# Softmax decode attention, forward and backward, on one core: the number of parts in which V of the first two head pairs is loaded

## The chip, the core and the metric

The kernel runs on one core of a Trainium2 chip. The metric is the device time of one execution in microseconds (us). The core has a matrix engine (PE, whose weight loads are listed as PEld), a vector engine (DVE), a scalar engine (ACT), a general engine (POOL) and a sync engine (SP) that here does nothing but start transfers. Transfers between the chip's main memory (DRAM, HBM) and the on-chip buffers are carried by 16 DMA engines.

## What is computed

One query row per head attends to 8192 keys, and the gradients of that are returned as well:

```python
B, H, Sq, Skv, Dh = 1, 32, 1, 8192, 128          # all bf16

def _fwd_reference(q, k, v):
    scale = q.shape[-1] ** -0.5
    scores = jnp.einsum('bhqd,bhkd->bhqk', q, k) * scale
    attn = _softmax(scores, axis=-1)
    return jnp.einsum('bhqk,bhkd->bhqd', attn, v)

def reference(q, k, v, grad_out):
    _out, _vjp = jax.vjp(_f, q, k, v)      # _f is _fwd_reference
    return (_out, *_vjp(grad_out))         # out, dq, dk, dv
```

K and V are read (134 MB together) and dK and dV, which have the same size, are written. dK is the outer product of the gradient of the scores (a number per key) with q, dV that of the softmax weights with grad_out.

## The kernel before

The 32 heads are taken as 16 pairs. K of a pair, 4 MB, lies in one buffer `Kt` of 128 partitions by 128 slots by 128 numbers; a slot is 256 bytes, so each partition holds 32 KB. V lies in the same way in `Vt`. There are three buffers for K (`K_BUFS`) and two for V (`V_BUFS`). The results overwrite the inputs: line 290 writes dV of a pair into its V buffer and dK into its K buffer, and stores carry the buffers to DRAM. A buffer is loaded again only when its stores have landed.

For each pair j the loop from line 355 on makes the scores with K (`k_blocks`, `k_scores`), the softmax, dK of the pair before, and then in eight steps r over sixteen slots each: transposes of V (`v_transposes`, line 215), the product of the softmax weights with V (`contract`, line 265), and dV (`outer`, line 290).

Transfers by the SP engine are issued in the order of the program: an issue that has to wait holds up all behind it. The order at the start is K of pair 0 (K0) in four parts, V0 in two, K1 in one, V1 in four, K2 in two (`LOADS`, lines 25 and 98 to 102). Then come the store of the second half of dV of pair 0 (line 299), the store of dK of pair 0 (line 305), the load of V2 (line 93; it goes into the buffer of V0, so it waits for all of dV of pair 0 to be stored), the two halves of dV of pair 1, and the load of K3. From there on it is one load and one store in turn, 4 MB each.

A transfer of 128 partitions is cut into packets of one partition each: 32 KB when the pair's buffer is moved in one part, 16 KB for a half, 8 KB for a quarter. Each of the 16 DMA engines has eight partitions of it.

The first half of dV of pair 0 (the slots below `SHARED`) is not stored by SP but by POOL, through a second queue (q0 in the profile; SP's is q1). `share_out` (lines 116 to 121) starts six stores, one for each entry of `SHARES`: the first engine, the first partition and the number of partitions, every third of them, in pieces of 8 KB. Before each it starts a tiny transfer (`turned`, line 111) that moves the place at which the next store begins among the engines. The entries give the 16 engines different amounts: between none and 24 pieces of 8 KB.

```python
def share_out(dst, src):
    for engine, first, n in SHARES:
        turn_to(engine)
        last = first + 3 * n - 2
        nc.gpsimd.dma_start(dst[first:last:3], src[first:last:3], max_dma_last_dim=8192)
```

Of the kernel before, what the change touches and what calls it, by code (L numbers as in the profile page):

```python
# [21 lines left out]
K_BUFS = 3  # L22
V_BUFS = 2
QD = 32
LOADS = {("k", 0): 4, ("v", 0): 2, ("v", 1): 4, ("k", 2): 2}
SHARED = 64
SHARES = ((6, 12, 39), (5, 2, 42), (5, 1, 8), (15, 55, 25), (10, 25, 10), (7, 0, 4))
GP = 4
# [3 lines left out]
def kernel(  # L32
# [50 lines left out]
    def load_k(j):  # L83
        parts = LOADS.get(("k", j), 1)
        Kt[j] = kpool.tile([P, NT, D], BF16, tag="K", name="Kt")
        for c in range(parts):
            nc.sync.dma_start(slots(Kt[j], c, parts), rows_of(k, j, c, parts))

    def load_v(j):
        Vt[j] = vpool.tile([P, NT, D], BF16, tag="V", name="Vt")  # L90
        parts = LOADS.get(("v", j), 1)
        for c in range(parts):
# [432 lines left out]
```

## Time and profile before

| what | value |
|---|---|
| time, median of 3 runs | 632.92 us (632.18 to 633.14) |
| time of the profiled execution | 632.87 us |
| its span on the core | 631.1 us |
| PE busy | 462.9 us (73%) |
| DVE busy | 516.4 us (82%) |
| ACT busy | 205.1 us (32%) |
| DMA traffic | 268.98 MB in 12164 packets, mean 426 GB/s |
| read from and written to HBM | 134.23 MB each |

The span is the time from the first to the last event that the profiler records on the core; the time of the execution is 1.8 us longer. Lines of the profile name the engine, the line of the program (L93 is line 93), the operation, and what is written from what (`Vt<-in_v_dram` is a load of V). "SPq" and "POOLq" are the sequencers that start transfers.

### The profile page before, as it was taken

To read this page: it belongs to the slowest core of one execution; us is meant where nothing else is said; L and a number is where in the kernel's file an instruction comes from. 1 tells how busy PE (TensorE), PEld (TensorE's weight loads), DVE (VectorE), ACT (ScalarE), POOL (GpSimd) and SP (SyncE) were. 2 spreads that over 40 slices of the span, in tenths; PEclk is the share of its full clock that TensorE was granted. 3 is DMA by queue.
4 is the path that set the end of the run, shared out by engine and by line. 5 is a ranking of instruction groups with operands and counts; after the bars stand their busy time and mean duration, and the time that the engine had idled before them with its cause. 6 is when DMAs were issued, how large, how long until landed. Compare 5 with 4: busy or idle time off the path is not lost.

```text
span 631.1 us, 8018 instructions
## 1 busy us (share of the span) xinstructions
PE 462.9 (73%) x3256; PEld 245.9 (39%) x3256; DVE 516.4 (82%) x654; ACT 205.1 (32%) x460; POOL 11.3 (2%) x23
## 2 busy tenths in 40 slices
PE   4887678878787788676888757867679776697671
PEld 1443344244443425233363432624336243262441
DVE  6579997989889798796879959879697895987973
ACT  2432424043342505134052330613316142160431
POOL 2040000000000000000000000000000000000000
PEclk9789987789798977788868789777897778987785
DMA  8999999999999999999999999999999999999997
GB/s 366 433 402 436 430 428 431 429 427 440 433 427 436 436 431 433 433 432 429 429 432 429 427 433 427 433 432 418 431 430 437 436 431 425 436 427 431 428 426 336
DMA packets 12164, 268.98 MB, mean 426 GB/s; under 512 B 1856, under 2 KB 1888, under 8 KB 1888
## 3 DMA queue, kind: packets, MB, share of 16 engines
q1 hardware_dynamic: 11232, 266.34, 98.5%
q0 software_dynamic: 800, 2.12, 0.8%
q8 instruction: 25, 0.41, 0.2%
q14 instruction: 11, 0.09, 0.0%
q10 hardware_dynamic: 96, 0.02, 0.0%
HBM read 134.23 MB, written 134.23 MB: 425 GB/s over the span
## 4 chain that ended last, share of the span: by engine, by line
issue 91%; DMA 3%; PE 3%; DVE 1%; ACT 0%; POOL 0%; POOLq 0%; ACTq 0%
DMA out_dram<-Vt 2%; PE s_ps L198 1%; DMA Kt<-in_k_dram 1%; PE T_ps L215 1%; PE acc_p L265 0%; DVE XK_sb L188 0%; DVE Vt L290 0%; POOL out_dram L120 0%; DVE q_blk L174 0%; ACT p_rep L452 0%; DVE sT L205 0%; ACT win L255 0%; ACT e L440 0%; POOL turned L111 0%; POOLq L520 0%
## 5 line engine op out<-in xcount | busy, mean ns | idle before, releaser
L198 PE MATMUL s_ps<-XK_sb,q_win 128*128 128x512 bf16 x512 | 152.4, 432 | 66.6 <-DVE XK_sb L188 61.3
L290 DVE TENSOR_TENSOR Vt<-p_rep,qd 128x2048 bf16<-128x2048 bf16 x128 | 154.0, 1223 | 40.1 <-PE acc_p L265 32.2
L188 DVE STREAM_TRANSPOSE XK_sb<-Kt 128x1024 f32<-128x1024 f32 x128 | 150.2, 1218 | 37.7 <-DMA Kt<-in_k_dram 35.0
L215 PE MATMUL T_ps<-ident_f,Vt 128*128 128x128 f32 x1024 | 165.4, 314 | 6.1 <-DMA Vt<-in_v_dram 6.1
L220 ACT COPY XV_sb<-T_ps 128x512 f32<-128x512 f32 x256 | 139.6, 591 | 82.6 <-PE T_ps L215 82.4
L290 DVE TENSOR_TENSOR Kt<-ds_rep,qd 128x2048 bf16<-128x2048 bf16 x128 | 149.5, 1215 | 3.2 <-PE acc_ds L265 2.8
L215 PEld LDWEIGHTS T_ps<-ident_f,Vt 128*128 128x128 f32 x1024 | 131.2, 160 | 43.8 <-issue 18.7
L198 PEld LDWEIGHTS <-q_win 128*128 128x128 bf16 x512 | 51.6, 110 | 155.6 <-issue 123.9
L265 PE MATMUL acc_p<-Vt,win 128*32 128x512 bf16 x512 | 55.9, 439 | 2.8 <-ACT win L255 2.8
L440 ACT ACTIVATE e<-sT,nbias 128x128 f32<-128x128 f32 x16 | 8.2, 515 | 150.6 <-DVE nbias L436 150.6
L265 PEld LDWEIGHTS <-win 128*32 128x32 bf16 x1024 | 23.0, 99 | 60.6 <-issue 49.4
L265 PE MATMUL acc_ds<-Kt,win 128*32 128x512 bf16 x512 | 42.7, 429 | 4.6 <-ACT win L255 4.6
L232 PE MATMUL dp_ps<-XV_sb,do_win 128*32 128x512 bf16 x512 | 34.3, 383 | 13.5 <-ACT XV_sb L220 13.5
L255 ACT COPY win<-ds 64x128 bf16<-64x128 bf16 x32 | 9.5, 296 | 106.4 <-DVE ds L327 106.2
L232 PEld LDWEIGHTS <-do_win 128*32 128x32 bf16 x512 | 14.3, 94 | 29.2 <-issue 22.5
L441 PE MATMUL m_ps<-rs,ones_f 128*128 128x1 f32 x32 | 7.5, 305 | 24.4 <-ACT e L440 24.4
L427 PE MATMUL m_ps<-ident_f,top 128*128 128x128 f32 x16 | 4.8, 300 | 23.5 <-DVE top L425 23.5
L205 DVE STREAM_TRANSPOSE sT<-s_ps 128x512 f32<-128x512 f32 x16 | 11.5, 717 | 10.7 <-PE s_ps L198 10.7
L441 PEld LDWEIGHTS m_ps<-rs,ones_f 128*128 128x128 f32 x32 | 6.2, 242 | 27.6 <-ACT e L440 27.6
L452 ACT ACTIVATE p_rep<-e,rinv 128x512 bf16<-128x512 f32 x16 | 11.5, 722 | 13.3 <-DVE rinv L450 13.3
L427 PEld LDWEIGHTS m_ps<-ident_f,top 128*128 128x128 f32 x16 | 2.1, 133 | 31.0 <-issue 25.4
L317 PEld LDWEIGHTS m_ps<-pd,ones_f 128*128 128x128 f32 x32 | 8.2, 276 | 10.6 <-DVE prod L248 9.8
(60 smaller groups left out, 158.1 us busy)
## 6 DMA issues: line engine op xcount, KB each, us to landing
Kt<-in_k_dram SPq DMA_DIRECT2D x14, 4096.0 KB, 29.1
Vt<-in_v_dram SPq DMA_DIRECT2D x14, 4096.0 KB, 29.0
out_dram<-Kt SPq DMA_DIRECT2D x13, 4096.0 KB, 25.1
out_dram<-Vt SPq DMA_DIRECT2D x13, 4096.0 KB, 32.3
out_dram<-Vt SPq DMA_DIRECT2D x5, 2048.0 KB, 16.2
out_dram<-Kt SPq DMA_DIRECT2D x5, 2048.0 KB, 15.7
Kt<-in_k_dram SPq DMA_DIRECT2D x4, 1024.0 KB, 8.2
Vt<-in_v_dram SPq DMA_DIRECT2D x2, 2048.0 KB, 17.5
```

What stands on the lines that cost most here:

```text
L188: nc.vector.transpose(XK[j, u][:].rearrange("p g w i -> p (g w i)"), slots(Kt[j], u, NU).rearrange("p g d -> p (g d)").bitcast(F32))
L198: nc.tensor.matmul(st[j]["s"][:], lhsT=q_win[:, c, at:at + P], rhs=cols[:, c // 2, c % 2], start=(u == 0 and c == 0), stop=(u == NU - 1 an ...
L205: nc.vector.transpose(sT[:].rearrange("p g r -> p (g r)"), x["s"][:])
L215: nc.tensor.transpose(T_ps[:, i, :], words[:, m * P:(m + 1) * P], ident_f[:])
L220: nc.scalar.copy(XV[j][:, b * TB:(b + 1) * TB, :], st[j].pop(("T", c))[:])
L232: nc.tensor.matmul(out[b * QD:(b + 1) * QD, :], lhsT=do_win[:, b // 2, e2, at:at + QD], rhs=cols[:, z, e2, :, b * QD:(b + 1) * QD], start= ...
L255: nc.scalar.copy(win[t * M:(t + 1) * M, :, at:at + 4], src[t * M:(t + 1) * M])
L265: nc.tensor.matmul(acc[which][b * QD:(b + 1) * QD, :], lhsT=win[:, g, at:at + QD], rhs=X[:, 4 * g:4 * g + 4, :].rearrange("p n d -> p (n d)"),
L290: nc.vector.tensor_tensor(slots(G, r, NU).rearrange("p n (a b) -> p n a b", b=R), slots(rep, r, NU).unsqueeze(2).to_broadcast([P, CH, D // ...
L317: nc.tensor.matmul(x["m"][:, 1:3], lhsT=ones_f[:], rhs=x["pd"][:], start=True, stop=True, skip_group_check=True)
L441: nc.tensor.matmul(x["m"][:, 0:1], lhsT=ones_f[:], rhs=rs[:], start=True, stop=True, skip_group_check=True)
L452: nc.scalar.activation(x["p"][:], e[:].unsqueeze(2).to_broadcast([P, NT, R]), ACT.Copy, scale=rinv[:])
```

## The change

```diff
-LOADS = {("k", 0): 4, ("v", 0): 2, ("v", 1): 4, ("k", 2): 2}
+LOADS = {("k", 0): 4, ("v", 0): 4, ("v", 1): 2, ("k", 2): 2}
```

V0 is loaded in four quarters (512 packets of 8 KB) where it was two halves (256 of 16 KB), and V1 in two halves where it was four quarters. The number of transfers, of packets and of bytes of the two together stays what it was. The order of the instructions on PE, DVE, ACT and POOL is the same; on SP the two loads exchange their numbers of issues, so that the single issue of K1 comes two issues later.

## The prediction, made before the changed kernel had run

> **What bounds the kernel now.** I read the page first: the row of DMA and the queue table.
>
> ```profile
> DMA  8999999999999999999999999999999999999997
> GB/s 366 433 402 436 430 428 431 429 427 440 433 427 436 436 431 433 433 432 429 429 432 429 427 433 427 433 432 418 431 430 437 436 431 425 436 427 431 428 426 336
> q1 hardware_dynamic: 11232, 266.34, 98.5%
> ```
>
> The 16 DMA engines are full in all slices but the first and the last; no other engine is (DVE, the next, has 82%). I also added up the trace's packet records, which give queue, start, duration and size: after the first packets at 2.0 us no engine is idle until the first has finished everything at 626.6 us. So the time is the DMA work. Moving work between other engines costs nothing, and an idle microsecond on the DMA engine that finishes last costs one microsecond. The 16 engines end between 626.6 and 630.1 us (the completion marks of the last stores); span 631.1, time 632.87, 0.05 below the median of the runs.
>
> Second, the order of SP's issues and what they wait for, because the engines stay full only while SP issues in time:
>
> ```profile
> 38.77 0.35 SPq L299 DMA_DIRECT2D out_dram<-Vt  x1
> 52.89 0.34 SPq L305 DMA_DIRECT2D out_dram<-Kt  x1
> 65.04 0.34 SPq L93 DMA_DIRECT2D Vt<-in_v_dram  x1
> 73.17 4.87 SPq L305 DMA_DIRECT2D out_dram<-Vt  x2
> 78.14 0.67 SPq L87 DMA_DIRECT2D Kt<-in_k_dram  x1
> ```
>
> ```profile
> SPq L93 <- DMA out_dram<-Vt: 11.7, 3, 6.1
> ```
>
> These are the times of issue, and from the table of waits (50 to 80 us) the line of V loads. V2's load goes out at 65.04 after a wait for stores of dV of pair 0 (dV0). Ahead of it in the queue there is then nothing but the store of dK of pair 0 (dK0, issued at 52.89). Behind it on SP stand the two halves of dV1 and the load of K3.
>
> Third, the DMA issues up to 60 us with their time to landing:
>
> ```profile
> out_dram<-Kt SPq DMA_DIRECT2D x1, 4096.0 KB, 21.9
> out_dram<-Vt SPq DMA_DIRECT2D x1, 2048.0 KB, 26.2
> ...
> out_dram<-Vt POOLq DMA_DIRECT2D x1, 64.0 KB, 17.3
> ```
>
> SP's half of dV0 lands at 38.77 + 26.2 = 65.0: this releases V2. POOL's last share, issued at 45.80, lands at 63.1, only 1.9 us before. dK0 lands at 74.8, and it covers V2's issue. A transfer of 64 KB that takes 17 us is the line to stop at. Why so long is seen in the queue counts of two windows, 37 to 48 us and 49 to 58 us:
>
> ```profile
> q1 hardware_dynamic: 382, 3.20, 69.8%
> q0 software_dynamic: 380, 1.45, 32.3%
> ```
>
> ```profile
> q1 hardware_dynamic: 233, 3.41, 89.0%
> q0 software_dynamic: 226, 0.42, 12.0%
> ```
>
> q0 is POOL's queue, q1 SP's (packets, MB, share). Whether SP's packets are mostly 8 KB (V1, first window) or 16 KB (K2, second), there is about one packet of q0 for each of q1, while the bytes are far from equal. So the engines take the two queues in turn, packet by packet: the share-out's pace is one packet per packet of SP. Larger packets on SP slow it.
>
> **The change part by part.** *V0 in four parts.* SP's issues early on each wait for the landing of the transfer eight before (the waits of K1 on the q row, of V1's parts on the grad row and three parts of K0, of K2 on K0 and V0). With two more issues ahead, K1 would go out at about 5.8 instead of 4.24, when K0's first part has landed, V1 at 8.2 and 10.6, K2 at 13.1 and 15.5. K0 and V0 keep the queue full until 22.8, so all are in time. PE takes V0 from 20.73 on and its second half from 31.98, and shows no wait for it. Price 0; the cover is some 17 us of queued work. Packets of 8 KB take 0.309 us, of 16 KB 0.611: 256 more here and 256 fewer in V1 cancel.
>
> *V1 in two parts* has the same zero for its users: the first half is used at 46.49 and has landed by 39.7, or a bit earlier with the change. But it is what SP's queue moves when the share-out begins. Step by step, per DMA engine:
>
> Before. POOL's first packet begins at 36.2; 12.4 of V1's 32 packets have begun by then (199 over 16 engines). Left on q1 until dV0's half is done: 19.6 of V1, 16 of K2, 8 of dV0 = 43.6. POOL's queue holds 256 pieces of 8 KB and 368 of 4 bytes (marks and fillers; a record of 8 bytes goes with one of these) = 624, or 39 turns. In the records from 36.2 to 59 us there are 613 packets of q1 to 585 of these: 1.05 each, so 39 turns take 41 packets, 2.6 short of 43.6; three 16 KB packets (1.83 us) do lie between the last mark of q0 (63.01) and the last of dV0's half (64.84). The count fits.
>
> After. The same bytes of V1 have moved at 36.2, that is 6.2 of 16 packets. Left until the end of dV0's half: 9.8 + 16 + 8 = 33.8. The share-out needs 39 to 41, so 5.2 to 7.2 turns are left, and what is next on q1 is dK0 with 32 KB packets of 1.213 us. I take 5.7, nearer the lower end, since some of the 5% are moments in which q0 was not ready for 0.3 us, which a packet of 0.6 us hides. POOL's two last shares wait for the first two to land (41.53 and 45.80 now) and go out about 2 and 5 us later, while some 15 turns still stand in the queue; no price.
>
> So on the engines with most of the share-out, whose part of dV0's half ends at 64.8 in both kernels (the same work in another order), the share-out ends at 64.8 + 5.7 x 1.22 = 71.8. V2's load is issued 0.2 later, 72.0, instead of 65.04. Its first packet comes 1.4 after the issue, as for the first K load (issued 0.74, first packets 1.99 to 2.6): 73.4.
>
> The cover: dK0's sixteen completion marks lie at 67.5, 70.5, then eleven from 71.3 to 73.0 and four from 74.4 to 74.6. The first to be done is the engine with nothing of the share-out. It would stand idle from 67.5 to 73.4, 5.9 us, the next 2.9, most 0.4 to 2.1, the last four not at all. What is late next: dV1's first store (73.17) stands behind V2 and is just not held up. PE's transposes of V2 wait 0.4 us for its landing at 84.2, which the last engines set; these lose nothing.
>
> What 5.9 us on one engine cost at the end: I followed its marks from transfer to transfer. It takes 9.70 to 10 us for most 4 MB transfers where the others take 9.68, so its lead of 3 us is gone by about 345 us, and it ends at 629.1, 1.0 before the last. The sum: 5.9 - 1.0 = 4.9 us later. Against the profiled time 632.87 + 4.9 = **637.8 us**. Nothing wins it back: no DMA engine is idle later.
>
> Bounds: each turn more or less is 1.22 us. With 4 turns 635.7; with 7.2 639.6; if all eight packets of dK0 pass first, 640.6, and about a microsecond more if the first packets after the stop are as long as the first of the run (0.6 to 1.1 us for 0.31). With 2.8 turns 634.2, 0.2% above 632.87; with 1.7 nothing is left.
>
> The Trainium skill (DMA: Bandwidth & Descriptors, "Queues, rings and completion order") says that a DMA engine changes between queues after a whole packet of typically 9 to 17 descriptors. By that the 39 turns would be through in three to five changes, the size of SP's packets would not matter, and the sum would be 632.9. The two windows above, with as many packets of q0 as of q1, speak against it, unless the 1:1 is chance.
>
> **The rivals.** (a) *The share-out isn't paced by SP's packets*: its 1:1 comes from how fast POOL's pieces become ready, about one in 0.6 us per engine. Then it still ends at about 63, dV0's half releases V2 at 65, and the time is 632.9. For it: 0.62 us is the turn in both windows (0.309 + 0.309 with data, 0.611 with a mark). Against: in the second window the pieces are nearly all marks of some 9 ns, long issued, and still wait one 16 KB packet each. It decides from 2.8 turns down; this is the case on the other side, not slower.
>
> (b) *The stretch in which stores set in gets cheaper.* From 30 to 40 us the rate is 377 and 374 GB/s instead of some 430: 1.3 us lost, with V1's packets at 0.42 us on the mean from about 35 to 37 us. If that is a cost per packet, half as many save half, 0.6 us; with (a) this gives 632.3, at most 631.6. Against: the bytes in flight are the same.
>
> (c) *The share-out outlasts dK0* on some engine: V2 goes out at about 75, all engines run dry, dV1's stores and K3 come late with it, 641 us. For it: engines with 41 or more turns exist in the records (three packets left there, up to six elsewhere).
>
> That the change doesn't change the packets can be excluded: the parts are separate issues of 8192 and 4096 numbers per partition.
>
> **Chances.** Forecast 0.73, (a) 0.12, (b) 0.05, (c) 0.10. The forecast's own range is 635.7 to 639.6 (4 to 7.2 turns). For 8 in 10 I go on to 640.6 at the top (eight turns), and down to 634.2 (2.8 turns), where (a) begins. About 0.2% (1.3 us) is what a measurement of this kernel can tell from no change; (a) and most of (b) lie within. Faster 0.03, the same 0.14, slower 0.83.
>
> **What would show it.** In the profile after: V2's load (L93) issued at 70 to 74 instead of 65.04, its wait for dV0's stores longer by that, with POOL's last share landing last; q0 packets in the window 66 to 72, where there were none; POOL's shares 5 and 6 issued at about 43.5 and 51; DMA share below 0.9 somewhere in 68 to 76, and 16 completion marks at the end spread over 8 us instead of 3.5, with a lower last slice. Wrong it would be if V2's issue stays at 65, or if it moves and the end does not (then some engine's idle time was free).

## The result, and the profile after

The changed kernel takes 638.97 us (median of 6 runs, 636.35 to 639.55) where the kernel before, run beside it, takes 632.69 (6 runs, 632.18 to 633.18): ratio of the means 1.0088, 95% interval 1.0073 to 1.0102. The profiled execution took 639.43 us with a span of 637.6.

The page of the changed kernel, the same rows:

```profile
DMA  8999999999999999999999999999999999999995
GB/s 362 430 418 431 384 396 430 437 425 438 429 435 428 427 433 434 429 434 429 433 427 434 429 432 429 429 438 427 439 426 433 430 427 431 434 439 429 420 422 241
q1 hardware_dynamic: 11232, 266.34, 97.7%
```

Traffic and packets are what they were. The rate is lower in two places: the fifth and sixth slice (64 to 96 us: 384 and 396 GB/s) and the last (241 instead of 336). The row of tenths hides the first of them.

Two words for what follows. A mark is the record of 4 bytes with which a transfer ends on an engine, so each transfer has 16. Times of packet records and marks, here and in the prediction, are counted from a zero 0.24 us before that of the rows of issues; differences between records are not touched by it.

SP's issues, and the wait of V2's load:

```profile
39.03 0.35 SPq L299 DMA_DIRECT2D out_dram<-Vt  x1
53.14 0.34 SPq L305 DMA_DIRECT2D out_dram<-Kt  x1
71.22 0.34 SPq L93 DMA_DIRECT2D Vt<-in_v_dram  x1
73.63 4.87 SPq L305 DMA_DIRECT2D out_dram<-Vt  x2
78.60 0.39 SPq L87 DMA_DIRECT2D Kt<-in_k_dram  x1
```

```profile
SPq L93 <- DMA out_dram<-Vt: 17.5, 1, 17.5
```

Of these issues one has moved by more than 0.5 us: V2's, by 6.2 us. Its wait has grown from 11.7 to 17.5 us. What it waits for is seen in the transfers issued up to 60 us (size, time to landing) and in POOL's last two shares:

```profile
out_dram<-Kt SPq DMA_DIRECT2D x1, 4096.0 KB, 21.6
out_dram<-Vt SPq DMA_DIRECT2D x1, 2048.0 KB, 26.0
...
out_dram<-Vt POOLq DMA_DIRECT2D x1, 400.0 KB, 25.8
...
out_dram<-Vt POOLq DMA_DIRECT2D x1, 64.0 KB, 20.6
```

```profile
42.76 0.56 POOL L120 DMA_DIRECT2D out_dram<-Vt  x1 [5.59 <-DMA out_dram<-Vt]
...
50.46 0.59 POOL L120 DMA_DIRECT2D out_dram<-Vt  x1 [5.86 <-DMA out_dram<-Vt]
```

SP's half of dV0 lands at 39.03 + 26.0 = 65.0, as before. POOL's last share, issued at 50.46, lands at 71.1, where it was 63.1: the share-out now releases V2. dK0 lands at 53.14 + 21.6 = 74.7, as before, but V2 is no longer queued behind it in time. The queue counts from 66 to 72 us show the share-out beside dK0's 32 KB packets, and the windows after it the hole (columns: window, length, busy time and number of instructions of five engines, granted clock, DMA share, GB/s):

```profile
q1 hardware_dynamic: 71, 2.06, 79.9%
q0 software_dynamic: 38, 0.05, 2.6%
```

```profile
66.00:70.00 4.00, 2.52 (x27) 1.01 (x25) 2.85 (x5) 2.98 (x8) 0.00 (x0) 0.65 0.95 406
70.00:72.00 2.00, 2.00 (x16) 0.82 (x8) 2.00 (x3) 0.34 (x1) 0.00 (x0) 0.50 0.63 258
72.00:74.00 2.00, 2.00 (x14) 1.58 (x10) 2.00 (x3) 0.83 (x2) 0.00 (x0) 0.50 0.91 279
```

In the kernel before, q0 has no packet in this stretch and the three windows moved 426, 463 and 401 GB/s. From 72 to 74 us the engines are 91% busy and move 279 GB/s: V2's first packets are slow. In the packet records, 13 of the packets that begin from 72.4 to 74.8 take 1.7 to 2.2 us instead of 1.21.

### The profile page after: what moved, and what is told of

Same layout as the page of the kernel before. It is cut to its first block, busy times and chain, and to the rows that moved or that the text cites. A ratio compares the mean times of both kernels' runs of the same rounds, so it can differ in the third digit from the quotient of the medians.

```text
span 637.6 us, 8018 instructions
## 1 busy us (share of the span) xinstructions
PE 463.3 (73%) x3256; PEld 247.8 (39%) x3256; DVE 516.2 (81%) x654; ACT 205.1 (32%) x460; POOL 11.1 (2%) x23
## 4 chain that ended last, share of the span: by engine, by line
issue 90%; DMA 3%; PE 3%; DVE 1%; ACT 0%; POOL 0%; POOLq 0%; ACTq 0%
DMA turned<-in_k_dram 3%; PE s_ps L198 1%; DMA Kt<-in_k_dram 1%; PE T_ps L215 1%; PE acc_p L265 0%; POOL out_dram L120 0%; DVE XK_sb L188 0%; DVE Vt L290 0%; DVE q_blk L174 0%; ACT p_rep L452 0%; DVE sT L205 0%; ACT win L255 0%; ACT e L440 0%; POOL turned L111 0%; POOLq L520 0%
## 5 line engine op out<-in xcount | busy, mean ns | idle before, releaser
L198 PE MATMUL s_ps<-XK_sb,q_win 128*128 128x512 bf16 x512 | 154.1, 438 | 69.3 <-DVE XK_sb L188 64.5
L265 PE MATMUL acc_ds<-Kt,win 128*32 128x512 bf16 x512 | 41.3, 417 | 4.6 <-ACT win L255 4.6
```

The costliest lines, as they stand in the source:

```text
L198: nc.tensor.matmul(st[j]["s"][:], lhsT=q_win[:, c, at:at + P], rhs=cols[:, c // 2, c % 2], start=(u == 0 and c == 0), stop=(u == NU - 1 an ...
L265: nc.tensor.matmul(acc[which][b * QD:(b + 1) * QD, :], lhsT=win[:, g, at:at + QD], rhs=X[:, 4 * g:4 * g + 4, :].rearrange("p n d -> p (n d)"),
```

## The experiments

Each kernel was timed beside the kernel before; the ratio is to that. The issue time of V2's load comes from the one profiled execution of each kernel.

**Which part of the change.** V1 alone:

```diff
-LOADS = {("k", 0): 4, ("v", 0): 2, ("v", 1): 4, ("k", 2): 2}
+LOADS = {("k", 0): 4, ("v", 0): 2, ("v", 1): 2, ("k", 2): 2}
```

> V1 alone in two parts, V0 in two as before. Turn theory (POOL's store queue moves one packet for each packet of SP's queue, so V1's fewer packets leave about six turns to the 32 KB packets of dK0, V2's load goes out at 70 to 73 us, the engine without share-out work stands idle some 6 us): like the changed kernel, 636 to 640 us. Rival (the finer V0, which pushes K1's issue back by 2.4 us, has a part in it): V2's load is issued 1 us or more earlier than at 71.2 and the time is 634 to 636 us.

640.07 us (637.14 to 640.96), ratio 1.0108 [1.0083, 1.0133]; V2's load at 72.51. Not to be told from the changed kernel.

V0 alone:

```diff
-LOADS = {("k", 0): 4, ("v", 0): 2, ("v", 1): 4, ("k", 2): 2}
+LOADS = {("k", 0): 4, ("v", 0): 4, ("v", 1): 4, ("k", 2): 2}
```

> V0 alone in four parts, V1 in four as before. Turn theory: V2's load at 65.0 us, no engine idle, 632 to 633.5 us, no change. Rival (the finer V0 has a part in it): V2's load later than 66 us, 634 us or more.

633.24 us, ratio 1.0006 [0.9996, 1.0015]; V2's load at 65.11. The finer V0 costs nothing that can be measured; V1 alone makes the loss.

**Is it the packets that SP's queue moves beside the share-out?** The changed kernel with K2 in four parts, so that V1 keeps its large packets and K2 makes up for their number:

```diff
-LOADS = {("k", 0): 4, ("v", 0): 4, ("v", 1): 2, ("k", 2): 2}
+LOADS = {("k", 0): 4, ("v", 0): 4, ("v", 1): 2, ("k", 2): 4}
```

> The changed kernel with K2 in four parts of 8 KB packets instead of two of 16 KB. Turn theory: packets left on SP's queue when the share-out begins are 9.8 of V1, 32 of K2 and 8 of dV0's half, 49.8 and more than the 39 to 41 turns of the share-out, so it ends in good time before dV0's half; V2's load at about 65 us, 632 to 633.5 us: the loss is gone although V1 stays in two parts. Rival (something in V1's two parts themselves, their landing or the later issue of K1): V2's load stays at 70 us or later and the time at 636 to 640 us.

633.09 us, ratio 1.0008 [0.9998, 1.0017], and V2's load goes out in time:

```profile
65.48 0.34 SPq L93 DMA_DIRECT2D Vt<-in_v_dram  x1
```

The loss is gone with V1 still in two parts. The opposite, K2 in one part and V1 untouched:

```diff
-LOADS = {("k", 0): 4, ("v", 0): 2, ("v", 1): 4, ("k", 2): 2}
+LOADS = {("k", 0): 4, ("v", 0): 2, ("v", 1): 4, ("k", 2): 1}
```

> The kernel before with K2 in one part of 32 KB packets instead of two of 16 KB; V0 and V1 untouched. Turn theory: 19.6 packets of V1, 8 of K2, 8 of dV0's half are left, 35.6, so 3.4 to 5.4 turns go to dK0's packets; V2's load at 69 to 71.5 us, the first engine idle 3 to 5 us, with the slow first packets of a restart (about 1.6 us in the changed kernel) 635 to 639 us. Rival (the loss comes with V1's parts): no change, 632 to 633.5 us.

637.00 us, 635.12 to 640.88 in six runs, ratio 1.0077 [1.0046, 1.0108]. The loss comes without touching V1. The profiled execution, one of the shortest (635.28 us), has V2's load some 1.5 us earlier than expected:

```profile
67.48 0.34 SPq L93 DMA_DIRECT2D Vt<-in_v_dram  x1
```

Why this kernel varies by 5.8 us, more than any other here, was not settled: only one of its executions has a trace.

A larger dose, V1 in one part of 32 KB packets:

```diff
-LOADS = {("k", 0): 4, ("v", 0): 2, ("v", 1): 4, ("k", 2): 2}
+LOADS = {("k", 0): 4, ("v", 0): 2, ("v", 1): 1, ("k", 2): 2}
```

> The kernel before with V1 in one part of 32 KB packets. Turn theory: 4.9 packets of V1, 16 of K2 and 8 of dV0's half are left when the share-out begins, 28.9, so 10 to 12 turns would have to go beside dK0, which has only eight packets: the share-out outlasts dK0 on every engine, V2's load goes out at 74.5 to 76 us, the first engine is idle some 9 us and all others too, 640 to 644 us, more than the changed kernel. Rival (the delay comes with the change from four parts to fewer and has one size): 636 to 640 us, V2's load at 70 to 73 us.

643.84 us, ratio 1.0175 [1.0160, 1.0190]. Its issue of V2 and its windows:

```profile
75.49 0.34 SPq L93 DMA_DIRECT2D Vt<-in_v_dram  x1
```

```profile
72.00:74.00 2.00, 1.60 (x22) 0.57 (x22) 2.00 (x3) 0.85 (x3) 0.00 (x0) 1.00 0.28 98
74.00:76.00 2.00, 2.00 (x11) 0.87 (x10) 2.00 (x2) 0.34 (x2) 0.00 (x0) 1.00 0.00 0
```

Here all 16 engines stand still for two microseconds, as expected where the share-out outlasts dK0.

**Turns or bytes?** The same question from POOL's side: larger pieces in the changed kernel, smaller ones in the kernel before.

```diff
-            nc.gpsimd.dma_start(dst[first:last:3], src[first:last:3], max_dma_last_dim=8192)
+            nc.gpsimd.dma_start(dst[first:last:3], src[first:last:3], max_dma_last_dim=16384)
```

> The changed kernel with the share-out cut into pieces of up to 16 KB instead of 8 KB; the same bytes go to the same DMA engines. Turn theory: with half as many pieces the share-out needs some 25 turns per engine instead of 39, fewer than the 33.8 packets left on SP's queue, so V2's load goes out at about 65 us and the time is 632 to 634 us. Rival (the share-out is late because of its bytes, or because SP's larger packets take a larger share of the bytes): V2's load at 70 us or later, 636 to 640 us.

V2's load goes out at 64.86, in time; and the kernel takes 639.09 us, ratio 1.0102 [1.0085, 1.0118]. The step up to V2 held, the time did not. The records have 128 pieces and 48 fillers (records of 4 bytes in the place of a piece), 11 per engine where 14 were expected, so the pieces do not lie on the engines they were on. A second try changed all entries but the longest:

```diff
-            nc.gpsimd.dma_start(dst[first:last:3], src[first:last:3], max_dma_last_dim=8192)
+            nc.gpsimd.dma_start(dst[first:last:3], src[first:last:3], max_dma_last_dim=8192 if n == 25 else 16384)
```

> The changed kernel with pieces of up to 16 KB in all entries of the share-out but the one of 25 partitions, which keeps its 8 KB pieces; with 16 KB throughout that entry had come to lie on other DMA engines (11 pieces and fillers per engine where 14 were expected), so V2's load was in time (64.9 us) and one engine still ended 5 us behind. Turn theory: 30 turns per engine instead of 39, fewer than the 33.8 packets left on SP's queue, V2's load at about 65 us; and since every entry now gives the same engines the same bytes as in the kernel before, also 632 to 634.5 us. Rival (larger pieces cost the lead of that engine in some other way): V2's load at 65 us and 637 to 640 us. Rival (bytes, not turns, make the share-out late): V2's load at 68 us or later.

637.66 us, ratio 1.0081 [1.0066, 1.0096], V2's load at 65.96: the first rival. The trace does not name the engines, but one of them can be followed: its packets are regularly a little longer than the others' (below). In the kernel before it is the first of the 16 to finish the first half of dV1, with its mark at 82.2 us. With 16 KB throughout that mark lies at 88.7, and here at 87.0, or 6.5 and 4.8 us later; the two kernels take 6.3 and 4.7 us longer. It has lost its lead to the pieces, not to waiting, and in both kernels one engine ends late: in the second, the last marks are fifteen at 630.0 to 630.3 and one at 634.4. So the expectation that every entry would keep its engines most likely failed too. That is inferred: in the kernel before this engine, as far as its records can be followed, has 39 of 4 bytes in the share-out and not one piece, and 4.8 us are about eight packets of 16 KB at 0.611 us.

The clean test of turns against bytes therefore goes the other way, with pieces cut smaller in the kernel before and every piece where it was:

```diff
-            nc.gpsimd.dma_start(dst[first:last:3], src[first:last:3], max_dma_last_dim=8192)
+            nc.gpsimd.dma_start(dst[first:last:3], src[first:last:3], max_dma_last_dim=4096)
```

> The kernel before with the share-out in pieces of 4 KB instead of 8 KB; the loads are untouched, each entry keeps its partitions, its order and its DMA engines (39 x 4 x 2048 numbers where it was 39 x 2 x 4096). Turn theory: 56 turns for pieces and fillers instead of 28, and 11 others, 67 per engine, against 43.6 packets left on SP's queue up to the end of dV0's half and eight of dK0: the share-out outlasts dK0, V2's load goes out at 74 to 77 us, and the time is 639 to 645 us, as with V1 in one part. Rival (the share-out's bytes, or SP's large packets as such, set its end): V2's load at 65 to 67 us, 632 to 635 us.

643.16 us, ratio 1.0164 [1.0147, 1.0181], with the same loads and the same bytes. V2's issue, and the queues from 49 to 58 us:

```profile
75.17 0.34 SPq L93 DMA_DIRECT2D Vt<-in_v_dram  x1
```

```profile
q1 hardware_dynamic: 245, 3.52, 92.1%
q0 software_dynamic: 245, 0.28, 8.7%
```

Again about one for one (both counts take in records of 4 bytes). Bytes are ruled out: halving the pieces delays V2 as much as quartering V1's number of packets does.

**What is the lead of one engine worth?** The kernel before without the share-out, so that all engines get the same:

```diff
-SHARED = 64
+SHARED = 0
```

> The kernel before without the share-out: SP stores all of dV of pair 0 in one transfer, so POOL's queue has no store to wait for and all 16 engines get the same work. Theory of the leading engine (one DMA engine loses some 7 us on the others over the run and needs its lead of up to 5 us from the share-out): V2's load without delay by the share-out, no engine idle, and yet 636 to 638 us, with one engine ending some 5 us after most others. Rival (the lead has no worth; the changed kernel loses by the dry stretch as such, on all engines): 632 to 634 us.

636.44 us, ratio 1.0059 [1.0044, 1.0074]; V2's load at 63.95 and, by the packet records, the engines idle for 0.2 us each in all from 5 to 600 us. It loses 3.7 us nevertheless: eleven engines end at 627.7 to 629.4, three by 630.8, the last two at 632.2 and 633.1. The last windows:

```profile
625.00:630.00 5.00, 0.00 (x0) 0.00 (x0) 0.00 (x0) 0.00 (x0) 0.00 (x0) 0.50 0.69 291
630.00:635.00 5.00, 0.00 (x0) 0.00 (x0) 0.00 (x0) 0.00 (x0) 0.00 (x0) 0.50 0.05 23
```

The control, the changed kernel without the share-out:

```diff
-SHARED = 64
+SHARED = 0
```

> The changed kernel without the share-out: SP stores all of dV of pair 0. Turn theory: with nothing on POOL's queue, V1's packets hold nothing up, so it is as the kernel before without the share-out (636.4 us): 635.5 to 637.5 us, V2's load at about 64 us. Rival (V1 in two parts costs something by itself): 638 us or more.

636.52 us, ratio 1.0060 [1.0043, 1.0077], V2's load at 64.43: the same as without the share-out before. No cost of V1 in two parts is seen without POOL's queue beside it.

All of it by one count (left: packets of SP's queue per engine from the start of the share-out to the end of dV0's half, worked out as in the prediction; turns: those of the share-out; slow engine: its mark at the end of dV1's store, in the profiled execution, whose time stands behind it):

| kernel | turns | left | V2's load issued, us | slow engine, us | profiled, us | median, us |
|---|---|---|---|---|---|---|
| before | 39 | 43.6 | 65.04 | 87.3 | 632.87 | 632.69 |
| V0 in four | 39 | 43.6 | 65.11 | 87.5 | 633.18 | 633.24 |
| changed, K2 in four | 39 | 49.8 | 65.48 | 87.9 | 632.82 | 633.09 |
| changed, 16 KB pieces | 22 | 33.8 | 64.86 | 93.8 | 638.91 | 639.09 |
| changed, mixed pieces | 30 | 33.8 | 65.96 | 92.0 | 637.36 | 637.66 |
| before, K2 in one | 39 | 35.6 | 67.48 | 89.9 | 635.28 | 637.00 |
| changed | 39 | 33.8 | 71.22 | 94.0 | 639.43 | 638.97 |
| V1 in two | 39 | 33.8 | 72.51 | 95.1 | 640.96 | 640.07 |
| V1 in one | 39 | 28.9 | 75.49 | 98.2 | 643.47 | 643.84 |
| before, 4 KB pieces | 67 | 43.6 | 75.17 | 98.0 | 643.26 | 643.16 |
| before, no share-out | - | - | 63.95 | 91.3 | 635.99 | 636.44 |
| changed, no share-out | - | - | 64.43 | 91.6 | 636.44 | 636.52 |

V2 is late in just the kernels with more turns than packets left. The two with the larger pieces lose for the other reason, the place of the work among the engines. The column of the slow engine joins the two reasons. This engine is known in every trace by the load behind dV1: at least six of its eight packets of 32 KB there are longer than 1.213 us, and of any other engine at most two. In all twelve profiled executions the time is 544.7 to 545.8 us more than its mark, while the times themselves differ by up to 10.7 us. So the loss of each kernel is already there when this one engine is done with dV1. No kernel tried was faster than the one before.

## Why the prediction was right, and what it mis-sized

The forecast was 637.8 us; the median is 638.97 and the profiled execution 639.43. The mechanism is the one forecast, and the experiments above confirm its two halves separately. That the number comes so close is in part luck: V2's first packets begin at 72.4 instead of 73.4, 1.0 us too early for the sum, and this hides more than half of the 1.9 us by which slow packets were left out of it.

- *V0 in four parts, price 0*: shown by the run with V0 alone. K1's issue came at 6.66, not at about 5.8, without effect.
- *One packet for one packet*: 5.7 turns left over was a little high, though within the range given. The last mark of the share-out lies at 71.0, and (71.0 - 64.8) / 1.22 = 5.1. V2's load went out at 71.22 instead of 72.0.
- *The first engine idle for 5.9 us*: its part of dK0 ends at 66.8, and V2's first packets begin at 72.4: 5.6 us. (Of dK0's sixteen marks before, ten and not eleven lie from 71.3 to 73.0; nothing in the sum hangs on it.)
- *The restart*: this is the term that was too small. I let V2 start at full speed and put slow first packets, as about a microsecond, into the upper bound alone. V2's marks lie at 84.0 to 87.0 instead of 77.2 to 84.3. From 72.4 a 4 MB transfer at 9.70 us would end on the first engine at 82.1, so slow packets cost it 1.9 us more. From 40 to 90 us packets took 1.9 us per engine more above their usual 0.31, 0.61 and 1.21 than in the kernel before. About 0.7 of that comes with V2's first packets, 1.1 with its last ones: at 80.5 to 84.2 us, just before the engines pass to dV1's store, nine of them within 0.3 us, some thirty packets take 1.35 to 2.5 us. Both groups are in all four kernels in which most engines ran dry (changed, V1 in two, V1 in one, 4 KB pieces), 0.6 to 0.7 and 1.1 to 1.2 us per engine. With K2 in one part, where one engine alone stood idle, some 1.5 us, the last group is 0.3; in the other kernels no 4 us from 60 to 100 us have more than 0.12. So the slow last packets go with the dry stretch as well; why packets become slow in either place, no run shows.
- *The last four engines lose nothing*: wrong for the same reason; their marks of V2 come 2.0 to 2.7 us later, and PE's transposes wait 3.7 us for V2 instead of 0.4. What that alone costs was not separated.
- *5.9 less 1.0 at the end*: the last engine ends at 636.5 instead of 630.1, 6.4 later. The first engine's marks were 84.0 - 77.2 = 6.8 late after V2; less the 1.0 by which it had ended before the last one, that is 5.8, and 0.6 more was lost on the way. Thirteen of the 16 engines end at 631.1 to 631.2, the other three at 631.6, 633.9 and 636.5. The thirteen end together because the last part of dK15's store goes out at 624.96 instead of 620.34: up to six engines stand idle for it between 624 and 626 us. So "no DMA engine is idle later" does not hold at the very end, but it did no good to the engine that ends last, which had older work left. The profile after shows the one straggler in its last windows:

```profile
625.00:630.00 5.00, 0.00 (x0) 0.00 (x0) 0.00 (x0) 0.00 (x0) 0.48 (x1) 0.50 0.98 409
630.00:635.00 5.00, 0.00 (x0) 0.00 (x0) 0.00 (x0) 0.00 (x0) 0.00 (x0) 0.50 0.21 88
635.00:640.00 5.00, 0.00 (x0) 0.00 (x0) 0.00 (x0) 0.00 (x0) 0.00 (x0) 0.53 0.02 7
```

Up to 630 us nearly all engines are at work. The 21% of the next window are mostly the thirteen up to 631.2, and after 635 us 2% are left: 0.02 x 16 engines x 5 us is 1.6 us, the work of one engine, which sets the time.

Of the rivals, (a) falls with the table: V2's issue follows the number of packets on either queue. (b), a gain from fewer packets, is not seen: without the share-out the two kernels are alike within 0.1 us. (c), the share-out outlasting dK0, is what V1 in one part and the 4 KB pieces do, at 643 to 644 us, more than the 641 given; slow packets took 1.8 us per engine there too. The Trainium skill's rule (DMA: Bandwidth & Descriptors, "Queues, rings and completion order") of 9 to 17 descriptors per change of queue does not hold for these two queues: the counts are 245 to 245, and V2's issue follows the number of turns.

What stays open: why the executions of the changed kernel spread over 3.2 us and those with K2 in one part over 5.8, where the kernel before spreads over 1 to 2. A turn more or less is worth 1.2 us by the prediction's sum, and the restart may differ from time to time; no run tells these apart.

## What to carry to other kernels

Where two queues share the DMA engines and take turns packet by packet, as these two did, the time of the transfer with the smaller packets goes by its number of packets times the time of one of the other queue's; count both before making either larger. Then look for who waits for its last byte, and how much queued work covers that wait: here a wait of 6 us ran out the cover on most engines, and the loss at the end was that of the one that had needed its lead. This kernel, bound by DMA, ends with its slowest DMA engine, so a small unequal transfer placed early was worth 3.7 us at the end, and any stop of the engine that needed its lead takes them back.

## What the runs showed that was not expected

- The restart after a dry stretch is dear: some of V2's first 32 KB packets took 1.7 to 2.2 us instead of 1.21, and some of its last ones, before the engines passed to a store nearly together, again 1.35 to 2.5; some 1.8 us per engine in each of the four kernels in which most engines ran dry.
- One DMA engine loses some 0.02 us and 0.15 to 0.4 us in turn on successive 4 MB transfers all through the run, the others only now and then some. Without the share-out the kernel takes 3.7 us longer, and one engine ends last, 5.4 us behind the first.
- POOL's queue gives an engine that has no piece of a store a record of 4 bytes in the place of each piece. With 8 KB pieces the counts are 256 pieces and 368 records of 4 bytes, of which 176 are the marks of 11 transfers on 16 engines and 192 are left: 28 pieces or fillers on every engine. With 4 KB pieces it is 512 and 560, 56 on each. So a share of nothing takes as many turns as a full one.
- The form of the pieces (39 x 2 x 4096 or 39 x 8192 numbers) seems to decide which engines carry them, at the same partitions and bytes: worth 4.7 to 6.3 us here. The engines' numbers are not in the traces, so this is inferred from the marks of the slow engine.
